# Block A's work moved off the fours, and second parts of weights given to GpSimd, in a two-block attention kernel

## The chip, the cores and the metric

The kernel runs on one core of a Trainium2 chip. The metric is the device time of one execution in microseconds. The core's engines work in parallel, each through its own instructions in order: TensorE (PE, with its weight loads PEld), VectorE (DVE), ScalarE (ACT), GpSimd (POOL) and SyncE (SP), which here issues nearly all DMAs. They wait for each other by semaphores only.

## The reference

Two attention blocks over the same shapes (2048 rows, 640 features, 32 heads of 20), whose results stand side by side:

```python
def _A_ref(x, wqkv, wo):               # local, dilated: 8 keys a row, 2 apart
    qkv = (x @ wqkv).reshape(B, S, 3, H, Dh)...
    idx = pos[:, None] - arange(8) * 2
    logits = einsum("bhsd,bhswd->bhsw", q, k[idx]) * Dh ** -0.5     # masked where idx < 0
    o = einsum("bhsw,bhswd->bhsd", softmax(logits), v[idx])
    return o @ wo
def _B_ref(x, wqkv, wo):               # full attention
    scores = einsum("bhqd,bhkd->bhqk", q, k) * Dh ** -0.5
    return einsum("bhqk,bhkd->bhqd", softmax(scores), v) @ wo
return concatenate([a, b], axis=-1)
```

All inputs and outputs are float32.

## The kernel before

**Numbers as two parts.** A matrix product of float32 operands runs as three passes over a first part (the value rounded, `act.copy` into a float32r tile) and a second part (the rest, a subtraction `raw - first`). Each weight and each piece of x is therefore split once: a cast on ACT and a `tensor_tensor` subtraction on DVE, or on GpSimd where the code says `gp`. The subtraction reads two SBUF tiles.

**Stages**, in PE's order: (1) block A's q, k, v rows (0 to 163 us). (2) The *fours* (`b_quad`, 163 to 237 us): block B's q and k for the first 1024 rows, five rounds (`m` = 0 to 4), each two column blocks by two halves of the rows with seven half products instead of eight; a round yields four results (`n` = 0 to 3), and behind each result the loop counts one group and does side work: the next round's weight pair is cast, summed and split. (3) The first V stage, 16 groups of `v_group` (237 to 274 us): block B's v rows for x's first half, half a weight (320 columns) in groups 1 to 8, the other half in 9 to 16, while x's second half is loaded (`x_pair.load`) and split (`x_pair.base`). (4) The *products* (274 to 361 us): q and k of the second 1024 rows, again five rounds `m` of two row blocks `n` and two weights `j`, 20 groups; `m_parts` splits the next round's two weights. From group 9 on a step of `b_max` stands behind each group: score products whose maxima DVE takes straight from PSUM (tile `mx`). (5) The second V stage, 14 groups with maxima too (361 to 412 us). (6) The loop over 512 steps (32 units of 16) of block B's attention (412 to 1669 us), in which PE's matmuls, ACT's exponentials and DVE's maxima follow an order written out by hand (`UNIT`); the maxima of a unit are taken 24 steps ahead of its scores. (7) The end, without maxima.

**Block A's attention** runs on GpSimd beside all this: `a_attention` is a generator of 128 pieces, and each call of `next(a_work)` issues one: a piece of scores (a product with q, `akv<-akv,aq`, then four sums and one into `al`) or one of values (`akv<-akv,al` and two sums), and the fetches (`a_fetch`, two transfers of 320 KB, and one of q where a row tile begins) for the piece two ahead; the first call fetches three. In the stages, `piece(...)` names the groups behind which a piece stands. In the loop it is every fourth step, and one more wherever `i % 96 == 33`. A finished tile of 128 rows is turned at place 9 of a unit and multiplied by A's output weight in the unit's one slot `G`.

**What else stands in the queues.** `wide_raw` loads V's half weight into three `stg` tiles (there are three in all), `wide_parts` splits it. `WPair.load` puts the pair of an odd round into the tile `aot`, that of an even one into two `stg` tiles. SP's queue holds every DMA in program order: stores of results (`qb_d`, `kb_d`, `vb_d`), loads, and block A's fetches. In the first V stage a V result is evicted by ACT into one of four `ve` tiles, which come free when their store four groups before has landed; PE has four PSUM banks for these groups. In the loop the maxima of a unit pass from DVE's turn to a split on GpSimd (`mtr`), a store and a load (`bq<-mdr`) before the next unit's scores.

Of the kernel before, what the change touches and what calls it, by code (L numbers as in the profile page):

```python
# [65 lines left out]
def attention_pair(ctx, tc, xa, wqk_a, wv_a, wo_a, xb, wqk_b, wv_b, wo_b, oa, ob):  # L66
# [142 lines left out]
            split(u[:, 0, m:m + b - a], u[:, 1, m:m + b - a], src[:, a:b], "p", second)  # L209
        return t, [lambda a=a, b=b: piece(a, b) for a, b in PAIRS]  # L210

    def wide_raw(src):

        t = [sb.tile([128, 640], F32, tag="stg", bufs=3, name="stg") for _ in PAIRS]
        raw = [u[:, :(b - a) * 320].rearrange("p (k c) -> p k c", c=320) for u, (a, b) in zip(t, PAIRS)]
        for r, (a, b) in zip(raw, PAIRS):
            sp.dma_start(r, src[:, a:b])
        return raw

    def wide_parts(raw):  # L220
        w = [sb.tile([128, KC, 320], F32R, tag="w", bufs=4, name="ww") for _ in range(2)]
        for r, (a, b) in zip(raw, PAIRS):
            act.copy(w[0][:, a:b], r)
            dve.tensor_tensor(w[1][:, a:b], r, w[0][:, a:b].bitcast(F32), ALU.subtract)
        return w

    def wide_pieces(src, second=None):
# [578 lines left out]
    groups = 0  # L806

    def piece(*at):
        if groups in at:
            next(a_work, None)  # L810

    loads = []
    for m in range(5):
        w = pairs_w.pop()
        for n, _ in enumerate(b_quad(w, x_pair)):
            tick()
            groups += 1
            piece(6, 11, 16)
            if m < 4:
                if n == 0:  # L820
                    pairs_w = [WPair(*MS[m + 1], w_raws.pop(0))]
                    pairs_w[0].base()
                    if m < 3:
                        w_raws.append(WPair.load(*MS[m + 2], m))
                elif n == 1:
                    pairs_w[0].sums()
                elif n == 2:
                    pairs_w[0].split()
            elif n == 1:
                WV = wide_parts(raw_v)  # L830
            if m == 3 and n == 3:
                raw_v = wide_raw(wv_b[0])
    low()

    def max_rows(m4, m1, q, qc):
# [365 lines left out]
    x_pair = XPair(2)  # L1201
    WV = [WV]

    def m_parts(raw):
        w = [sb.tile([128, 2, KC, 128], F32R, tag="w", bufs=4, name="w") for _ in raw]
        for u, r in zip(w, raw):
            act.copy(u[:, 0], r)
            dve.tensor_tensor(u[:, 1], r, u[:, 0].bitcast(F32), ALU.subtract)
        return w

    w_raws, WB = [], []
    for groups in range(1, 17):
        half, s = divmod(groups - 1, 8)
        v_group(s // 4, half, s)
        tick()
        if groups == 1:
            raw_v = wide_raw(wv_b[1])
        elif groups == 6:
            WV.append(wide_parts(raw_v))
        if groups in (1, 2, 3, 4, 5):  # L1220
            x_pair.load(groups - 1)
        if groups in (9, 11):
            x_pair.base(groups // 2 - 4)
        if groups in (7, 9):
            w_raws.append(WPair.load(*MS[groups // 2 - 3], groups // 2 - 3))
        if groups == 13:
            WB.append(m_parts(w_raws.pop(0)))
        piece(3, 8, 13)
# [6 lines left out]
    for m in range(5):  # L1235
        w = WB.pop()
        for n in (2, 3):
            for j in range(2):
                p = bank()
                product(p, [lambda i, k=k: w[j][:, i, k] for k in range(KC)],  # L1240
                        [lambda i, k=k: chunk(XB[n], i, k) for k in range(KC)], True, True)
                give(p)
                b_parts(p, MS[m][j], n, None, False)
                tick()
                groups += 1
                if n == 2 and j and m < 4:
                    WB.append(m_parts(w_raws.pop(0)))
                elif n == 2 and m < 3:
                    w_raws.append(WPair.load(*MS[m + 2], m))
                elif (m, n, j) == (3, 3, 0):  # L1250
                    raw_v = wide_raw(wv_b[0])
                elif (m, n, j) == (4, 2, 0):
                    WV = [wide_parts(raw_v)]
                piece(2, 5, 8, 11, 14, 17)
                if groups == 14:
                    k_loads = b_keys(0, 2, 4)
                if groups in (1, 2, 14, 15):
                    for fn in k_loads[:2]:
                        k_loads.pop(0)()
                if groups > 2 and len(q_loads) > 8:  # L1260
                    for fn in q_loads[:2]:
                        q_loads.pop(0)()
                if groups > 17 and v_loads:
                    v_piece(0, *v_loads.pop(0))
                if groups > 8:
                    for i in islice(steps, 1):
                        b_max(i)
    v_late = [(3, 1, 14), (3, 1, 15)]
    for groups in range(1, 15):
# [2 lines left out]
        tick()  # L1272
        if groups == 1:
            raw_v = wide_raw(wv_b[1])
        elif groups == 5:
            WV.append(wide_parts(raw_v))
        for i in islice(steps, 1):
            b_max(i)
        if groups > 2 and q_loads:
# [49 lines left out]
    for i in range(NS + LAG):  # L1329
# [9 lines left out]
        tick()  # L1339
        if loads and i % 2:  # L1340
            loads.pop(0)()
        if i > 14 and (i % 4 == 3 or i % 96 == 33) and next(a_work, 0) == 0:
            for d in done_a:
                d[0] -= 1
        if i % NKB == SLOT and done_a and done_a[0][0] <= 0:
# [79 lines left out]
```

## Time and profile before

| | |
|---|---|
| median of 3 runs | 1785.26 us (1784.45 to 1787.24) |
| the profiled execution | 1786.85 us, span of its trace 1785.0 us |
| busy share: PE / DVE / ACT / POOL | 98% / 79% / 76% / 69% |
| PE busy in the fours | 67.3 of 74.2 us |
| PE busy in the first V stage | 35.8 of 37.2 us |
| PE busy in the products | 82.6 of 86.5 us |
| PE busy in the second V stage | 46.1 of 51.1 us |
| PE busy in the loop | 1248.8 of 1257.0 us |
| GpSimd busy in the loop | 1073.2 of 1257.0 us |

In a timeline a row is: start in us, duration in us, engine, line, operation, out<-in by tile names, shapes, the count of equal instructions merged (their duration is then the stretch that they cover), and in brackets the engine's idle time before it with what ended it. In a list of groups a row gives the count, the busy us and the mean ns of one, and the idle time before. All instructions pass through one helper line, L61, so they are told apart by tile names: `w`, `ww` weights of B, `xn`, `xl` the parts of x, `akv` block A's fetched rows, `pr` an evicted result of q or k, `mx` maxima.

### The profile page before, as it was taken

The page shows a single profiled execution, that of the slowest core. Times are in us where ns is not written, and L with a number is a line of the kernel's source. Part 1 is how long each engine was busy: PE and PEld are TensorE (multiplying, and loading weights), DVE is VectorE, ACT ScalarE, POOL GpSimd, SP SyncE. Part 2 cuts the span into 40 slices and gives each one's busy share as a digit, 9 for nine tenths or more (in the row PEclk, how much of TensorE's full clock was granted, in tenths as well). Part 3 has the DMA queues.
Part 4 walks back from the last instruction along what each step waited for, and adds up shares of the span by engine and source line. Part 5 has one row for each costly group of instructions (what it writes and reads, how often), then busy time and mean ns, then how long its engine had stood idle before and what let it go on. Part 6 is the DMA issues. An engine that isn't in the chain of part 4 may idle for free.

```text
span 1785.0 us, 32041 instructions
## 1 busy us (share of the span) xinstructions
PE 1754.0 (98%) x11301; PEld 995.6 (56%) x11301; DVE 1410.9 (79%) x1914; ACT 1348.8 (76%) x2632; POOL 1224.8 (69%) x1080
## 2 busy tenths in 40 slices
PE   9999899989999999999999999999999999999999
PEld 8987688676444445444444444445444444444569
DVE  3115844777999999999999999999999999999400
ACT  4224233117999998999999999998999999888881
POOL 0000555533899989899898998888989899845432
PEclk9999999999999999999999999999999999999999
DMA  7574688656435653564555456545553535221223
GB/s 257 165 239 159 232 293 274 213 167 171 141 117 161 168 152 104 171 161 141 155 146 153 127 173 159 154 123 163 142 175 96 140 104 163 64 72 55 66 70 110
DMA packets 215859, 272.04 MB, mean 152 GB/s; under 512 B 91894, under 2 KB 132214, under 8 KB 215698
## 3 DMA queue, kind: packets, MB, share of 16 engines
q1 hardware_dynamic: 215122, 269.34, 50.5%
q8 instruction: 89, 1.46, 0.4%
q14 instruction: 72, 0.59, 0.1%
q10 hardware_dynamic: 576, 0.66, 0.1%
HBM read 195.17 MB, written 74.74 MB: 151 GB/s over the span
## 4 chain that ended last, share of the span: by engine, by line
PE 78%; DVE 5%; ACT 2%; DMA 1%; issue 1%; SPq 0%; POOL 0%; DVEq 0%; ACTq 0%; POOLq 0%
PE ps_st L61 78%; DVE mx L61 4%; ACT e L61 1%; DMA stg<-wv_b 1%; SPq L61 0%; DVE w L61 0%; POOL braw L61 0%; DVE ww L61 0%; DMA stg<-wqk_b 0%; ACT more L61 0%; DVE pr L61 0%; ACT pr L61 0%; DMA bq<-mdr 0%; ACT ww L61 0%; ACT w L61 0%
## 5 line engine op out<-in xcount | busy, mean ns | idle before, releaser
L61 DVE TENSOR_REDUCE mx<-ps_st 128x1 f32<-128x512 f32 (+1 forms) x1500 | 1217.7, 877 | 67.0 <-PE ps_st L61 55.8
L61 ACT ACTIVATE e<-ps_st 128x512 f32<-128x512 f32 x2048 | 1067.4, 609 | 37.4 <-PE ps_st L61 17.8
L61 PE MATMUL ps_st<-bq,bk 62*128 62x512 f32 x2048 | 610.9, 440 | 1.8 <-DMA bq<-mdr 0.9
L61 PE MATMUL ps_st<-bk,bq 60*128 60x512 f32 x2048 | 557.7, 435 | 10.3 <-DVE mx L61 10.1
L61 PEld LDWEIGHTS ps_st<-bq,bk 62*128 62x128 f32 x2048 | 288.5, 184 | 480.3 <-ACT e L61 342.9
L61 PE MATMUL ps_st<-e,vb 128*32 128x512 f32 x4096 | 542.9, 604 | 2.7
L61 POOL TENSOR_TENSOR braw<-braw,more 128x512 f32<-128x512 f32 x224 | 287.7, 1284 | 130.4 <-ACT more L61 119.6
L61 POOL TENSOR_TENSOR akv<-akv,aq 128x1280 f32<-128x1280 f32 x64 | 189.4, 2959 | 200.8 <-DVE w L61 189.4
L61 POOL TENSOR_TENSOR akv<-akv 128x640 f32<-128x640 f32 (+3 forms) x304 | 288.5, 949 | 23.8
L61 PEld LDWEIGHTS ps_st<-bk,bq 60*128 60x128 f32 x2048 | 267.3, 184 | 46.5 <-DVE mx L61 21.0
L61 ACT COPY ro<-ps_st 128x320 f32<-128x320 f32 (+2 forms) x132 | 62.5, 475 | 193.6 <-PE ps_st L61 167.3
L61 PEld LDWEIGHTS ps_st<-e,vb 128*32 128x32 f32 x4096 | 82.0, 108 | 157.3 <-issue 71.3
L61 POOL TENSOR_TENSOR akv<-akv,al 128x1280 f32<-128x1280 f32 x64 | 151.4, 2366 | 0.2
L61 ACT COPY more<-ps_st 128x512 f32<-128x512 f32 x224 | 132.5, 591 | 1.4 <-PE ps_st L61 1.4
L61 PE MATMUL ps_st<-ww,xn 128*128 128x320 f32 x768 | 126.9, 315 | 2.2 <-ACT ww L61 1.2
L61 PEld LDWEIGHTS ps_st<-ww,xn 128*128 128x128 f32 x768 | 115.3, 190 | 19.4 <-ACT e L61 8.8
L61 PE MATMUL ps_st<-wc,xn 128*128 128x512 f32 (+1 forms) x432 | 101.8, 381 | 0.0
L61 PEld LDWEIGHTS ps_st<-wc,xn 128*128 128x128 f32 x432 | 80.4, 189 | 14.1 <-ACT xn L61 0.3
L61 PE MATMUL ps_st<-xn,w 128*128 128x512 f32 x330 | 85.9, 406 | 0.7 <-ACT ro L61 0.7
L61 PE MATMUL ps_st<-ww,aot 128*128 128x320 f32 x480 | 77.8, 314 | 1.6
L61 POOL TENSOR_TENSOR ao<-ao,akv 128x640 f32<-128x640 f32 x48 | 75.3, 1570 | 3.8
L61 PEld LDWEIGHTS ps_st<-ww,aot 128*128 128x128 f32 x480 | 70.6, 188 | 10.2 <-ACT e L61 3.8
(81 smaller groups left out, 1088.3 us busy)
## 6 DMA issues: line engine op xcount, KB each, us to landing
akv<-ka_d SPq DMA_DIRECT2D x128, 320.0 KB
akv<-va_d SPq DMA_DIRECT2D x128, 320.0 KB
wx<-wa_d SPq DMA_DIRECT2D x24, 480.0 KB
kb_d<-pr SPq DMA_DIRECT2D x20, 512.0 KB
qb_d<-pr SPq DMA_DIRECT2D x20, 512.0 KB
bq<-qb_d SPq DMA_DIRECT2D x64, 160.0 KB
bk<-kb_d SPq DMA_DIRECT2D x14, 640.0 KB
rb<-s_d SPq DMA_DIRECT2D x128, 64.0 KB
```

The costliest lines, as they stand in the source:

```text
L61: return self.tc.keep_in_program_order(op(*a, **k))
```

## The change

It has four parts.

1. `piece(6, 11, 16)` in the fours is gone, so that block A's first three pieces stand in the first V stage (behind groups 3, 8 and 13, where pieces four to six stood); the products get seven pieces (behind groups 1, 4, 7, ... 19) for six (2, 5, ... 17).
2. Second parts of weights by GpSimd: `m_parts(..., gp)` for the four pairs inside the products, issued behind the first result of a round's four instead of the second (`n == 2 and not j`), the pair's load one group later; `wide_parts(..., gp)` for V's two half weights in the second V stage, its second one group earlier. V's second half weight in the first V stage stays with DVE, two groups earlier (group 4 for 6).
3. V's first half weight is asked for behind round 3's first result instead of its fourth, two of its three pieces into the tile `aot`, and split behind round 4's first result instead of its second.
4. In the loop the additional piece comes every 72 steps instead of 96.

The core of the diff:

```diff
-    def wide_raw(src):
-        t = [sb.tile([128, 640], F32, tag="stg", bufs=3, name="stg") for _ in PAIRS]
+    def wide_raw(src, other=False):
+        t = []
+        if other:
+            u = sb.tile([128, 2, 640], F32, tag="aot", bufs=1, name="stg")
+            t = [u[:, 0], u[:, 1]]
+        while len(t) < len(PAIRS):
+            t.append(sb.tile([128, 640], F32, tag="stg", bufs=3, name="stg"))
...
-    def wide_parts(raw):
+    def wide_parts(raw, e=None):
...
-            dve.tensor_tensor(w[1][:, a:b], r, w[0][:, a:b].bitcast(F32), ALU.subtract)
+            (e or dve).tensor_tensor(w[1][:, a:b], r, w[0][:, a:b].bitcast(F32), ALU.subtract)
...
-            piece(6, 11, 16)
...
-            elif n == 1:
+            elif n == 0:
                 WV = wide_parts(raw_v)
-            if m == 3 and n == 3:
-                raw_v = wide_raw(wv_b[0])
+            if m == 3 and n == 0:
+                raw_v = wide_raw(wv_b[0], True)
...
-    def m_parts(raw):
+    def m_parts(raw, e=dve):
...
-            dve.tensor_tensor(u[:, 1], r, u[:, 0].bitcast(F32), ALU.subtract)
+            e.tensor_tensor(u[:, 1], r, u[:, 0].bitcast(F32), ALU.subtract)
...
-        elif groups == 6:
+        elif groups == 4:
             WV.append(wide_parts(raw_v))
...
-                if n == 2 and j and m < 4:
-                    WB.append(m_parts(w_raws.pop(0)))
+                if n == 2 and not j and m < 4:
+                    WB.append(m_parts(w_raws.pop(0), gp))
                 elif n == 2 and m < 3:
                     w_raws.append(WPair.load(*MS[m + 2], m))
...
-                    WV = [wide_parts(raw_v)]
-                piece(2, 5, 8, 11, 14, 17)
+                    WV = [wide_parts(raw_v, gp)]
+                piece(1, 4, 7, 10, 13, 16, 19)
...
-        elif groups == 5:
-            WV.append(wide_parts(raw_v))
+        elif groups == 4:
+            WV.append(wide_parts(raw_v, gp))
...
-        if i > 14 and (i % 4 == 3 or i % 96 == 33) and next(a_work, 0) == 0:
+        if i > 14 and (i % 4 == 3 or i % 72 == 33) and next(a_work, 0) == 0:
```

**Place one: from the fours into the first V stage.** GpSimd's rows behind its last memset of stage 1 (`zero`), before:

```order
L61 MEMSET zero 7x640
L61 TENSOR_TENSOR akv<-akv,aq 128x1280
L61 TENSOR_TENSOR akv<-akv 128x2x320
L61 TENSOR_TENSOR akv<-akv 128x2x160
L61 TENSOR_TENSOR akv<-akv 128x2x64
L61 TENSOR_TENSOR akv<-akv 128x2x32
L61 TENSOR_TENSOR al<-akv 128x64
```

and of the change (`mx` and `ve` are set at the end of the fours):

```order
L61 MEMSET zero 7x640
L61 MEMSET mx_1744 128x32
L61 MEMSET mx_1745 128x32
L61 MEMSET ve 128x347 x4
L61 TENSOR_TENSOR akv<-akv,aq 128x1280
```

SP's rows in the first V stage, from the store of the second V result on, before:

```order
L61 DMA vb_d<-ve 128x336
L61 DMA stg<-xb 128x2x512
L61 DMA vb_d<-ve 128x336
L61 DMA stg<-xb 128x1024
L61 DMA akv<-ka_d 128x640 x2
L61 DMA vb_d<-ve 128x336
```

and of the change:

```order
L61 DMA vb_d<-ve 128x336
L61 DMA stg<-xb 128x2x512
L61 DMA vb_d<-ve 128x336
L61 DMA stg<-xb 128x1024
L61 DMA aq<-qa_d 128x640
L61 DMA akv<-ka_d 128x640 x6
L61 DMA vb_d<-ve 128x336
```

The first piece moved behind the memsets of `ve`, out of the fours, and its seven transfers now stand ahead of the store of the fourth V result.

**Place two: the products.** DVE's rows around the first steps with maxima, before:

```order
L61 RECIPROCAL am<-am 128x32
L61 TENSOR_TENSOR pr<-ps_st,pr 128x512
L61 TENSOR_REDUCE mx_2392<-ps_st 128x2 x2
L61 TENSOR_TENSOR pr<-ps_st,pr 128x512
L61 TENSOR_TENSOR w<-stg,w 128x640 x2
L61 TENSOR_REDUCE mx_2392<-ps_st 128x2 x2
```

and of the change:

```order
L61 TENSOR_REDUCE am<-al 128x32
L61 TENSOR_TENSOR pr<-ps_st,pr 128x512 x2
L61 TENSOR_REDUCE mx_2362<-ps_st 128x2 x2
L61 TENSOR_TENSOR pr<-ps_st,pr 128x512
L61 TENSOR_REDUCE mx_2362<-ps_st 128x2 x2
```

GpSimd's rows there, of the change (before, only pieces stand there):

```order
L61 TENSOR_TENSOR al<-akv 128x64
L61 TENSOR_TENSOR w<-stg,w 128x640 x2
L61 TENSOR_TENSOR akv<-akv,aq 128x1280
L61 TENSOR_TENSOR akv<-akv 128x2x320
L61 TENSOR_TENSOR akv<-akv 128x2x160
```

The weight's two subtractions left DVE's row between an eviction and the maxima, and stand on GpSimd between two pieces.

**Place three: the loop, unit 6** (steps 96 to 111). GpSimd's rows ahead of the split of the next unit's maxima (`mtr`), before:

```order
L61 TENSOR_TENSOR braw<-braw,more 128x512
L61 TENSOR_TENSOR al<-al,am 128x256
L61 TENSOR_TENSOR akv<-akv,aq 128x1280
L61 TENSOR_TENSOR akv<-akv 128x2x320
L61 TENSOR_TENSOR akv<-akv 128x2x160
L61 TENSOR_TENSOR akv<-akv 128x2x64
L61 TENSOR_TENSOR akv<-akv 128x2x32
L61 TENSOR_TENSOR al<-akv 128x64
L61 TENSOR_TENSOR braw<-braw,more 128x512 x2
L61 CAST mtr<-mtr 128x32
```

and of the change (`braw` sums block B's outputs):

```order
L61 TENSOR_TENSOR al<-akv 128x64
L61 TENSOR_TENSOR braw<-braw,more 128x512
L61 TENSOR_TENSOR akv<-akv,aq 128x1280
L61 TENSOR_TENSOR akv<-akv 128x2x320
L61 TENSOR_TENSOR akv<-akv 128x2x160
L61 TENSOR_TENSOR akv<-akv 128x2x64
L61 TENSOR_TENSOR akv<-akv 128x2x32
L61 TENSOR_TENSOR al<-akv 128x64
L61 TENSOR_TENSOR braw<-braw,more 128x512
L61 CAST mtr<-mtr 128x32
```

The piece right ahead of the split is the additional one of step 105, and the regular piece of step 103 ends one sum ahead of it; before, the piece ahead of the split was that of step 103, with two sums of `braw` behind it.

PE's order is the same in both programs, and so are the steps at which A's outputs are multiplied in the loop.

## The prediction

> **What bounds the kernel now.** I read the stages first (the view of busy times by stretch), then the timeline of TensorE (PE) inside each short stage, then what ran on VectorE (DVE) and GpSimd (POOL) at each gap. The page has PE busy 98% of 1785.0 us, so a shorter time must come from PE's gaps or from matmuls that run slowly behind a gap. The stages ahead of the long loop are where those are:
>
> ```profile
> 163.00:237.20 74.20, 67.32 (x270) 51.48 (x270) 57.25 (x83) 24.22 (x46) 23.44 (x22) 0.95 0.59 206
> 237.20:274.40 37.20, 35.76 (x240) 35.27 (x241) 17.91 (x20) 16.65 (x31) 26.44 (x23) 1.00 0.89 312
> 360.90:412.00 51.10, 46.07 (x274) 38.53 (x273) 37.93 (x40) 7.91 (x19) 20.05 (x23) 0.93 0.58 175
> 412.00:1669.00 1257.00, 1248.77 (x8650) 587.46 (x8649) 1199.27 (x1644) 1155.97 (x2267) 1073.19 (x936) 1.00 0.48 136
> ```
>
> Columns are the stretch, its length, then PE, weight loads, DVE, ACT, POOL, the granted clock, the DMA share and GB/s. The fours (163 to 237) leave PE idle for 6.9 us and the second V stage (361 to 412) for 5.0, both at a lowered clock; the loop leaves 8 us in 1257. So I look for the change's effect in the 250 us ahead of the loop.
>
> **The fours.** A round of the fours starts with the same six matmuls, so the distance of those rows is the length of a round:
>
> ```profile
> 175.88 1.56 PE L61 MATMUL ps_st<-xn,w 128*128 128x512 f32 x6
> ...
> 189.06 1.56 PE L61 MATMUL ps_st<-xn,w 128*128 128x512 f32 x6
> ...
> 204.06 1.56 PE L61 MATMUL ps_st<-xn,w 128*128 128x512 f32 x6
> ...
> 223.83 1.56 PE L61 MATMUL ps_st<-xn,w 128*128 128x512 f32 x6
> ```
>
> 13.18, then 15.00, then 19.77 us. Block A's three pieces run exactly in the two long rounds, and what they do to DVE stands in these rows:
>
> ```profile
> 190.76 1.29 DVE L61 TENSOR_TENSOR w<-stg,w 128x512 fp32r<-128x512 f32 x2 [0.65 <-ACT w L61]
> ...
> 207.34 3.43 POOL L61 TENSOR_TENSOR akv<-akv,aq 128x1280 f32<-128x1280 f32 x1
> ...
> 208.65 4.62 DVE L61 TENSOR_TENSOR w<-stg,w 128x512 fp32r<-128x512 f32 x2 [0.65 <-ACT w L61]
> ```
>
> The same two subtractions take 1.29 us alone and 4.62 beside a piece: a subtraction whose two inputs both lie in SBUF waits out GpSimd's instruction. Without pieces each round should be 13.18: 1.82 + 6.59 = **8.4 us saved**. V's first weight, which the change has split one group earlier in the last round, costs nothing there: rounds with a weight pair being prepared (two casts, two subtractions and more at that same place) were 13.18 as well.
>
> **V's first weight.**
>
> ```profile
> 237.57 1.90 ACT L61 CAST ww<-stg 128x640 fp32r<-128x640 f32 x3 [1.74 <-DMA stg<-wv_b]
> ...
> 238.35 0.56 PE L61 MATMUL ps_st<-ww,xn 128*128 128x320 f32 x2 [1.17 <-ACT ww L61]
> ...
> 241.21 1.92 PE L61 MATMUL ps_st<-ww,xn 128*128 128x320 f32 x12
> ...
> 274.42 2.96 PE L61 MATMUL ps_st<-xn,w 128*128 128x512 f32 x12
> ```
>
> ACT waits for the transfer of wv_b and PE for ACT. Groups 2 to 16 take (274.42 - 241.21)/15 = 2.21 us each, the first 2.86. Asked for three groups earlier into tiles that are free by then, and split a group earlier, the weight is ready: 1.17 + 0.65 = **1.8 us saved**.
>
> **Second parts by GpSimd.** In the products a group is a matrix product, then two maxima tiles per DVE step:
>
> ```profile
> 302.42 2.96 PE L61 MATMUL ps_st<-xn,w 128*128 128x512 f32 x12
> ...
> 316.39 0.50 PE L61 MATMUL ps_st<-bk,bq 60*128 60x512 f32 x2 [1.61 <-DVE mx L61]
> 317.52 0.74 PE L61 MATMUL ps_st<-bk,bq 60*128 60x512 f32 x2 [0.63 <-DVE mx L61]
> 318.18 4.36 PE L61 MATMUL ps_st<-xn,w 128*128 128x512 f32 x12
> ...
> 323.84 3.05 PE L61 MATMUL ps_st<-xn,w 128*128 128x512 f32 x12
> ...
> 328.19 2.13 PE L61 MATMUL ps_st<-xn,w 128*128 128x512 f32 x8
> ...
> 360.87 2.03 PE L61 MATMUL ps_st<-ww,xn 128*128 128x320 f32 x12
> ```
>
> An undisturbed group is 328.19 - 323.84 = 4.35 us. Groups 9 to 20 take 360.87 - 302.42 = 58.45 for 12 x 4.35 = 52.2: 6.2 too many. The row at 316.39 names DVE's maxima, and these are late because of the weight's subtractions, ahead of them on DVE:
>
> ```profile
> 311.71 3.49 DVE L61 TENSOR_TENSOR w<-stg,w 128x640 fp32r<-128x640 f32 x2
> 315.12 2.34 DVE L61 TENSOR_REDUCE mx<-ps_st 128x2 f32<-128x1024 f32 x2
> ```
>
> DVE owes 2.34 for maxima in each 4.35 us, and the low part of an eviction before them; 3.49 more doesn't fit. What stays reads PSUM and shows no slowing beside pieces (2.34 here). **6.2 us saved**. In the second V stage it is the same with V's second weight:
>
> ```profile
> 376.62 2.03 PE L61 MATMUL ps_st<-ww,xn 128*128 128x320 f32 x12
> ...
> 377.19 5.23 DVE L61 TENSOR_TENSOR ww<-stg,ww 128x640 fp32r<-128x640 f32 x3 [1.39 <-ACT ww L61]
> ...
> 383.61 0.79 PE L61 MATMUL ps_st<-bk,bq 60*128 60x512 f32 x2 [4.52 <-DVE mx L61]
> ...
> 390.25 2.03 PE L61 MATMUL ps_st<-ww,xn 128*128 128x320 f32 x12
> ```
>
> Five groups from 360.87 to 376.62 take 3.15 each, the next two 390.25 - 376.62 = 13.63: **7.3 us saved**, the slow matmuls behind the gap included. Together 8.4 + 1.8 + 6.2 + 7.3 = **23.7**.
>
> **What comes in its place.** First, block A's first piece now starts in the first V stage, with three fetches at once: seven transfers of 320 KB where there were two, ahead of the fourth V store on SP's one queue. Behind that store waits ACT's eviction, behind the evictions the casts of x, then DVE's eight subtractions, then PE at 274.42:
>
> ```profile
> 260.50 0.43 ACT L61 COPY ve<-ps_st 128x320 f32<-128x320 f32 x1 [3.62 <-DMA vb_d<-ve]
> ...
> 263.46 3.86 DVE L61 TENSOR_TENSOR xn<-stg,xn 128x1024 fp32r<-128x1024 f32 x2 [4.95 <-ACT xn L61]
> ...
> 268.12 2.61 DVE L61 TENSOR_TENSOR xn<-stg,xn 128x1024 fp32r<-128x1024 f32 x2
> ...
> 271.25 1.55 DVE L61 TENSOR_TENSOR w<-stg,w 128x640 fp32r<-128x640 f32 x2
> ```
>
> Five more transfers at this stage's 312 GB/s are 5.2 us; the stage's stores and loads start some 2 us earlier against PE, since the evictions of the last round no longer wait behind V's weight. The delay of ACT lies between 0 and 5.2; I take half, 2.6. DVE: alone the eight take 4 x 1.3 + 2 x 0.65 (half the size) + 2 x 0.78 = 8.1 us; in the trace they took 272.80 - 263.46 = 9.3, since a piece ran beside the first four alone. Now three pieces stand back to back from the fetches' landing on, so all eight run beside one:
>
> ```profile
> 274.12 2.96 POOL L61 TENSOR_TENSOR akv<-akv,aq 128x1280 f32<-128x1280 f32 x1
> ...
> 280.97 2.96 POOL L61 TENSOR_TENSOR akv<-akv,aq 128x1280 f32<-128x1280 f32 x1
> ```
>
> A piece of scores, six instructions, is 280.97 - 274.12 = 6.85 us. By the row at 263.46 each subtraction beside one loses (3.86 - 2.61)/2 = 0.6: 8 x 0.6 = 5.0, less the 1.2 that stands there now, 3.8. The first half weight was done near 272.0, 2.4 ahead of PE. So PE waits 3.8 + 2.6 - 2.4 = 4.0. Behind 2.2 us of waiting (1.61 at 316.39, 0.63 at 317.52) a product took 4.36 instead of 3.05: 1.3 more. I take **5.3**. The lower bound is 0 (no delay, no new meeting). The upper has each subtraction behind a whole GpSimd instruction, a piece and the next one's product (6.85 + 2.96 = 9.8, less 1.2), and all of the delay: 8.6 + 5.2 - 2.4 + 1.3 = 12.7. I stay nearer the lower half, since 0.6 is the row of this very subtraction.
>
> The Trainium skill speaks against the change here: SBUF — State Buffer, "Who interferes with whom", has a DVE instruction with two SBUF inputs and a GpSimd instruction that reads SBUF exclude each other, whoever is second blocking to the end. By that alone the upper 8.6 would hold and the term be near 10, the time 1772; the trace agrees in the fours (4.62 for 1.29), while the 0.6 at 263.46 lies below it. On the slow matmuls, TensorE: Matmul & The Clock Gate, "Part 1: The HAM clock gate", lets the clock fall after an idle window of about 3.4 us, by which a wait of 4.0 in pieces would often cost no ramp and the 5.3 be 4.0; the row at 318.18 shows one after 2.2, and I keep it.
>
> Second, GpSimd's queue. Its prices:
>
> ```profile
> L61 POOL TENSOR_TENSOR akv<-akv,al 128x1280 f32<-128x1280 f32 x64 | 151.4, 2366 | 0.2
> ...
> L61 POOL TENSOR_TENSOR akv<-akv 128x640 f32<-128x640 f32 x112 | 176.6, 1577 | 8.8
> ...
> L61 POOL TENSOR_TENSOR ww<-stg,ww 128x640 fp32r<-128x640 f32 x8 | 12.9, 1610 | 0.6
> ```
>
> A piece of values, a product and two sums of 640, is 2.37 + 2 x 1.58 = 5.5 us. The products' 80.2 us get 5 x 6.9 + 2 x 5.5 + 4 x 3.2 + 4.1 for V's = 62 us of GpSimd: it fits. The tight place is the second pair handed over. An estimate of where GpSimd stands: the fetches are asked for at V's third group, 6.6 us into the stage, behind V's second weight and three loads of x (2.4 MB, 7.7 us at 312 GB/s), and are 2.3 MB themselves (7.3), so the pieces start 14 to 20 us into the 37.2 and take 3 x 6.85 and half of DVE's 8.1: they end 2 to 8 us into the products. Then come the first pair (3.2), two pieces (13.7) and half of the second pair (1.6), done at 20 to 27, where PE asks for it at group 9, (302.42 - 274.42) = 28.0. Bounds 0 and 3 (the other half); I take **0.5**, near 0, since the halves are wanted one group apart. Third, the loop. It gets 115 pieces for 113, extra ones at steps 33, 105, 177, ...; each second of these falls on the step right ahead of GpSimd's split of the next unit's maxima (place three of the order). What lateness costs there:
>
> ```profile
> 521.40 0.21 DVE L61 STREAM_TRANSPOSE mtr<-mx 128x32 f32<-128x32 f32 x1
> ...
> 528.75 0.20 POOL L61 CAST mtr<-mtr 128x32 fp32r<-128x32 f32 x1
> ...
> 536.66 0.49 PE L61 MATMUL ps_st<-bq,bk 62*128 62x512 f32 x1 [0.93 <-DMA bq<-mdr]
> ```
>
> Behind the extra piece at step 33 GpSimd was 7.1 us late and PE waited 0.93, so up to 6.2 are free, and one piece is 6.9 or 5.5. Six extra pieces now, five before: between -1 (waits like this one vanish, as the pieces there are of values now) and +3 (1 us at three places); I take **0.5**.
>
> **The sum** on the profiled execution's own 1786.85 us (span 1785.0 and 1.85 around it): -23.7 + 5.3 + 0.5 + 0.5 = -17.4, 1769.4. It lies 1.6 above the median of the runs shown, 1785.26, within their spread; from the median the forecast is **1767.9**.
>
> **Rivals.** (1) Nothing new waits in the V stage and at the products' start (the train of transfers is drained in time): 1785.3 - 23.7 + 1 = 1762.6, down to 1760. For it: the stores start earlier. Against: DMA share 0.89 there already. (2) GpSimd becomes the bound in the products, since its pieces are lengthened by DVE at the start and every later pair is late by what remains: another 5 to 9 us (twice the backlog of up to 8, less what the 18 us of room give back), 1773 to 1777. For it: 62 us of 80 and that backlog. Against: the handovers behind the second come four groups of 4.35 apart, 17.4 us for one pair and at most 1.4 pieces. (3) The change doesn't do what it says in the fours, since their long rounds have another cause (206 GB/s of transfers, say): 8.4 stays, 1776.3. Against: DVE's two durations. (4) Slower: GpSimd falls behind in the loop at the three places where an extra piece now stands right ahead of the split of the maxima (steps 105, 249, 393), and the next unit's scores wait for the maxima. To eat 17.4 us each must hold PE for 5.8, so the split must be 5.8 + 6.2 = 12 us late; with both scores pieces there still queued, 13.7, it is 7.5 each, 22, and the time 1790. Against: 7.1 is what the trace shows behind an extra piece; two of the three places have pieces of values; GpSimd is idle for 184 of the loop's 1257 us.
>
> **How the numbers follow.** Forecast 0.58 (1763 to 1773), rival 1 0.16, rival 2 0.14, rival 3 0.07, rival 4 0.05. 1759.5 to 1776 takes in the first two and most of rival 2, over eight in ten. The terms' own bounds are -23.7 - 1 (1760.5) and -23.7 + 12.7 + 3 + 3 (1780); the last 4 us of that would need all three at their worst, and I leave them out. A measurement of this kernel tells 0.2% (3.6 us) from no change. Faster than that: everything but rival 4 and the tail of rivals 2 and 3, 0.91; within it 0.04; slower 0.05.
>
> **What would show it.** In the fours all rounds 13.2 us apart and no DVE w above 1.3 for two; V's first group 2.2; in the products no gap ended by DVE mx, no w or ww on DVE after the first pair; the second V stage at some 3.1 a group. A PE gap ended by DVE w or xn at the products' start, of 2 to 6 us, would show the new wait; its absence, rival 1; gaps ended by POOL w at later pairs, rival 2; units of the loop above 42 us with PE released by DMA bq<-mdr, rival 4. The forecast is wrong if the stages ahead of the loop shorten by less than 12 or more than 25 us, or if the loop from its first values product on grows by more than 3.

## The result, and the profile after

The changed kernel takes 1766.8 us (median; 1764.1 to 1772.1) beside 1785.2 for the kernel before on the same chip: a ratio of 0.990, 95% interval 0.987 to 0.992. The forecast was 1767.9, the range 1759.5 to 1776.0. The profiled execution took 1767.61 us, its span is 1765.8, so its span is 19.2 shorter than that of before. The busy times by stretch, cut at the same instructions of PE in both traces (first matmul of the fours, of the first V stage, of the products, of the second V stage, first values product of the loop, and that of unit 30 and 31), first before:

```profile
163.28:238.35 75.07, 67.32 (x271) 51.48 (x271) 57.27 (x84) 24.66 (x46) 23.44 (x22) 0.95 0.60 209
238.35:274.42 36.07, 35.77 (x240) 35.28 (x241) 17.88 (x20) 15.93 (x30) 26.46 (x23) 1.00 0.88 309
274.42:360.87 86.45, 82.57 (x350) 60.19 (x348) 51.16 (x54) 19.17 (x33) 44.69 (x34) 0.98 0.72 239
360.87:417.11 56.24, 51.21 (x307) 42.25 (x305) 40.97 (x45) 11.42 (x27) 20.15 (x24) 0.94 0.58 167
417.11:1653.69 1236.58, 1228.73 (x8523) 577.99 (x8521) 1180.98 (x1621) 1137.86 (x2231) 1060.55 (x924) 1.00 0.48 137
1653.69:1700.46 46.77, 46.03 (x316) 25.73 (x315) 17.79 (x26) 41.87 (x85) 20.45 (x21) 1.00 0.19 55
```

and after:

```profile
162.56:227.84 65.28, 64.64 (x271) 50.22 (x271) 49.29 (x87) 25.55 (x48) 0.71 (x2) 1.00 0.51 184
227.84:263.04 35.20, 35.20 (x242) 35.20 (x240) 13.68 (x13) 14.97 (x28) 15.77 (x12) 1.00 0.96 339
263.04:346.07 83.03, 80.52 (x350) 58.97 (x348) 45.90 (x49) 19.16 (x34) 72.04 (x63) 1.00 0.78 258
346.07:395.03 48.96, 48.79 (x307) 40.33 (x305) 36.30 (x41) 11.42 (x27) 25.83 (x23) 1.00 0.74 211
395.03:1631.67 1236.64, 1229.96 (x8522) 576.71 (x8521) 1182.05 (x1622) 1137.68 (x2231) 1075.37 (x939) 1.00 0.49 138
1631.67:1681.22 49.55, 47.66 (x316) 26.05 (x314) 19.40 (x26) 41.91 (x85) 20.47 (x21) 0.97 0.17 52
```

| stretch | before | after | difference | forecast |
|---|---|---|---|---|
| fours and first V stage | 111.1 | 100.5 | -10.7 | -8.4 - 1.8 |
| products | 86.45 | 83.03 | -3.4 | -6.2 + 5.3 + 0.5 |
| second V stage | 56.24 | 48.96 | -7.3 | -7.3 |
| loop up to unit 30 | 1236.58 | 1236.64 | +0.1 | +0.5 |
| unit 30 | 46.77 | 49.55 | +2.8 | none |

The last 84.5 us differ by 0.04; stage 1, which the change doesn't touch, came out 0.7 shorter. In the timeline of PE after, the rounds of the fours and the first V group stand so:

```profile
188.35 1.56 PE L61 MATMUL ps_st<-xn,w 128*128 128x512 f32 x6
...
201.53 1.56 PE L61 MATMUL ps_st<-xn,w 128*128 128x512 f32 x6
...
214.67 1.56 PE L61 MATMUL ps_st<-xn,w 128*128 128x512 f32 x6
...
227.84 1.93 PE L61 MATMUL ps_st<-ww,xn 128*128 128x320 f32 x12
...
230.04 1.92 PE L61 MATMUL ps_st<-ww,xn 128*128 128x320 f32 x12
```

Every round is 13.2 us, the V stage begins without a wait and its first group takes 2.20. At the products' start stands the new wait. PE, DVE and ACT there:

```profile
263.04 0.62 PE L61 MATMUL ps_st<-xn,w 128*128 128x512 f32 x2
266.08 2.59 PE L61 MATMUL ps_st<-xn,w 128*128 128x512 f32 x10 [2.42 <-DVE w L61]
...
269.21 2.96 PE L61 MATMUL ps_st<-xn,w 128*128 128x512 f32 x12
```

```profile
254.01 5.22 DVE L61 TENSOR_TENSOR xn<-stg,xn 128x1024 fp32r<-128x1024 f32 x2 [14.07 <-ACT xn L61]
...
265.10 4.42 DVE L61 TENSOR_TENSOR w<-stg,w 128x640 fp32r<-128x640 f32 x2
```

```profile
251.04 0.43 ACT L61 COPY ve<-ps_st 128x320 f32<-128x320 f32 x1 [7.13 <-DMA vb_d<-ve]
```

The first product takes 269.21 - 263.04 = 6.17 us for 3.49 elsewhere: 2.7 lost. ACT waited 7.13 for a store behind the seven transfers, and DVE's eight subtractions run beside pieces from 254.0 to 269.5. Two of the pieces' rows on GpSimd:

```profile
254.21 3.94 POOL L61 TENSOR_TENSOR akv<-akv,aq 128x1280 f32<-128x1280 f32 x1
...
265.31 3.53 POOL L61 TENSOR_TENSOR akv<-akv,aq 128x1280 f32<-128x1280 f32 x1
```

From group 9 on the products keep 4.35 a group but for one loss of 0.34.

The 2.8 of unit 30 were in no term. GpSimd after, then DVE after:

```profile
1639.97 1.55 POOL L61 TENSOR_TENSOR ww<-stg,ww 128x640 fp32r<-128x640 f32 x1
```

```profile
1640.02 2.05 DVE L61 TENSOR_TENSOR xl<-stg,xl 128x512 fp32r<-128x512 f32 x1
```

Before, the same two met the other way round: DVE's `xl` began 0.12 ahead of GpSimd's, took 0.69, and GpSimd's took 1.98. Whoever begins second waits: in eleven of the twelve profiles that have both instructions DVE's began first, by 0.04 to 0.27 us, and GpSimd's took 1.87 to 2.07 for 1.55; this one is the twelfth. Here 0.05 us decided, and DVE's maxima came late. PE after:

```profile
1642.73 0.49 PE L61 MATMUL ps_st<-bk,bq 60*128 60x512 f32 x1 [1.19 <-DVE mx L61]
```

Of the 2.8, some 1.2 are this wait and 1.6 are matmuls that ran more slowly in this unit, whose clock was 0.97. PE's other wait there, 0.69 for maxima, is no part of the loss, since it was 0.73 before.

### The profile page after: what moved, and what is told of

The parts are those of the page before. It is cut to its first block, busy times and chain, and to the rows that moved or that the text cites. A ratio compares the mean times of both kernels' runs of the same rounds, so it can differ in the third digit from the quotient of the medians.

```text
span 1765.8 us, 32044 instructions
## 1 busy us (share of the span) xinstructions
PE 1748.4 (99%) x11301; PEld 989.7 (56%) x11301; DVE 1391.4 (79%) x1900; ACT 1348.6 (76%) x2632; POOL 1239.4 (70%) x1094
## 4 chain that ended last, share of the span: by engine, by line
PE 86%; DVE 6%; POOL 2%; ACT 2%; DMA 2%; issue 1%; SPq 1%; DVEq 0%; POOLq 0%; ACTq 0%
PE ps_st L61 86%; DVE mx L61 5%; POOL akv L61 1%; ACT e L61 1%; SPq L61 1%; DMA vb_d<-ve 1%; DMA akv<-ka_d 0%; POOL braw L61 0%; DVE pr L61 0%; DMA bq<-mdr 0%; DVE stg L61 0%; DVE xl L61 0%; ACT more L61 0%; ACT pr L61 0%; DMA qb_d<-pr 0%
## 5 line engine op out<-in xcount | busy, mean ns | idle before, releaser
L61 POOL TENSOR_TENSOR akv<-akv 128x640 f32<-128x640 f32 (+3 forms) x304 | 284.0, 934 | 23.8
```

The source lines that it names most:

```text
L61: return self.tc.keep_in_program_order(op(*a, **k))
```

## The experiments

### Each half of the change alone

First parts 1 and 4 on the kernel before: the pieces move, the weights stay.

```diff
-            piece(6, 11, 16)
...
-                piece(2, 5, 8, 11, 14, 17)
+                piece(1, 4, 7, 10, 13, 16, 19)
...
-        if i > 14 and (i % 4 == 3 or i % 96 == 33) and next(a_work, 0) == 0:
+        if i > 14 and (i % 4 == 3 or i % 72 == 33) and next(a_work, 0) == 0:
```

> Parts 1 and 4 alone on the kernel before: no piece beside the fours, seven in the products, an extra one every 72 steps; all weights as before. Theory (the terms of the sum stand side by side and add up): the four full rounds of the fours 13.2 us apart (8.4 saved), V's first group still 2.9, a wait of PE for DVE at the products' start as in the change (2.7 there), groups 9 to 20 of the products still near 58 and the second V stage still near 51. Time 1785.3 - 8.4 + 2.7 = 1779.6, between 1777 and 1782. Rival (the long rounds of the fours come from the weights' work, not from the pieces): long rounds stay, 1785 to 1788.

Measured: 1785.2 us (1779.5 to 1790.5), ratio 0.999 (0.997 to 1.001): by the median nothing, a miss by 5.6. The ten executions lie in two groups, though: five at 1779.5 to 1783.7, four of them where the theory had the time, and five at 1786.8 to 1790.5. The profile is of one of the second group (1790.2). In it the rounds are 13.2 as expected, but the products take 96.5 us for 86.5: 4.7 more in the first product, where 2.7 had been expected, and 5.5 more in groups 9 to 20. PE there:

```profile
268.93 3.74 PE L61 MATMUL ps_st<-xn,w 128*128 128x512 f32 x10 [2.92 <-DVE w L61]
...
312.81 0.50 PE L61 MATMUL ps_st<-bk,bq 60*128 60x512 f32 x2 [2.44 <-DVE mx L61]
...
350.11 0.50 PE L61 MATMUL ps_st<-bk,bq 60*128 60x512 f32 x2 [3.37 <-DVE mx L61]
```

and DVE ahead of the two later waits:

```profile
307.30 4.32 DVE L61 TENSOR_TENSOR w<-stg,w 128x640 fp32r<-128x640 f32 x2
...
343.34 5.58 DVE L61 TENSOR_TENSOR ww<-stg,ww 128x640 fp32r<-128x640 f32 x3
```

In this execution the pieces met DVE's subtractions of weights again, now in the products (4.32 for two, where a pair alone takes 1.6), and what the fours gained went there and into the wait at the start. The five faster executions have no profile. Their median, 1780.3, is 5.4 below the kernel before, and the theory had 5.7 (8.4 - 2.7), so there the loss in the products can't have been as large. Their mean granted clock was 0.995 to 0.998, that of the others 0.992 to 0.995. The rival (the fours' rounds stay long) is out.

Then parts 2 and 3 alone: in the changed kernel the pieces go back to their old places.

```diff
+            piece(6, 11, 16)
...
-                piece(1, 4, 7, 10, 13, 16, 19)
+                piece(2, 5, 8, 11, 14, 17)
...
-        if i > 14 and (i % 4 == 3 or i % 72 == 33) and next(a_work, 0) == 0:
+        if i > 14 and (i % 4 == 3 or i % 96 == 33) and next(a_work, 0) == 0:
```

> Parts 2 and 3 alone: second parts by GpSimd, V's first weight asked for earlier; the pieces at their old places (three in the fours, six in the products, every 96 steps in the loop). Theory: fours' rounds 15.0 and 19.8 again where pieces run, V's first group 2.2, no PE wait for DVE at the products' start, products' groups 4.35 and second V stage's 3.1 from the first to the last: 1785.3 - 1.8 - 6.2 - 7.3 = 1770.0, between 1768 and 1773. Rival (GpSimd can take the second parts only because the pieces moved: with a piece behind group 2 and 5 instead of 1 and 4 a pair is late): PE gaps ended by GpSimd's w at groups 5 or 9 of the products, 3 to 7 us each, 1773 to 1780.

Measured: 1771.6 us (1770.4 to 1772.3), ratio 0.991 (0.990 to 0.993): 14.0 saved. Rounds in PE's timeline:

```profile
203.96 1.56 PE L61 MATMUL ps_st<-xn,w 128*128 128x512 f32 x6
...
223.71 1.56 PE L61 MATMUL ps_st<-xn,w 128*128 128x512 f32 x6
```

Both long rounds are there again (14.96, and the 19.75 shown), the products have 80.1 us and the second V stage 48.8, and no wait of PE for GpSimd's weights stands in the products: the rival is out. By their medians the halves give 0.4 and 14.0, 14.4 together, and the whole change 18.4: in the median the 8.4 of the fours are had only where the weights have left DVE. With the faster five executions of the first half the terms would add up (5.4 + 14.0 = 19.4).

### What made the fours' rounds long

The changed kernel with three pieces' work put back on tiles that GpSimd fills itself, so without transfers:

```diff
+            if groups == 5:
+                dummy = sb.tile([128, 2, D], F32, tag="akv", bufs=4, name="akv")
+                dq = sb.tile([128, D], F32, tag="aq", bufs=2, name="aq")
+                dl = sb.tile([128, WIN, H], F32, tag="al", bufs=2, name="al")
+                for u in (dummy, dq):
+                    gp.memset(u, 1.0)
+                a_t[-1] = [dq, dl, None]
+            if groups in (6, 11, 16):
+                a_scores(-1, 1, dummy)
```

> The changed kernel with three pieces' worth of GpSimd work added back in the fours at the old places, on tiles that GpSimd filled itself, so that no transfer belongs to it (six instructions of the same sizes each; they add to no result). Theory (DVE's subtractions wait for GpSimd's instructions): rounds of the fours are long again, DVE's pair of subtractions 3 to 5 us where it meets a piece instead of 1.3; 4 to 9 us lost there, time 1771 to 1776. Rival (transfers made them long): all rounds 13.2, time that of the change, 1766 to 1768.

Measured: 1768.9 us (1766.1 to 1770.8), all rounds 13.2. That looks like the rival, but the trace says that the experiment missed its place. GpSimd:

```profile
122.39 2.96 POOL L61 TENSOR_TENSOR akv<-akv,aq 128x1280 f32<-128x1280 f32 x1
```

With nothing to wait for, GpSimd ran these instructions in stage 1, 120 to 148 us, not beside the fours. So the work was tied to the third round by one column that it reads of a weight split there:

```diff
+            if groups == 7:
...
+                gp.tensor_copy(dq[:, :1], pairs_w[0].y[:, 1, 0, :1].bitcast(F32))
+                for _ in range(3):
+                    a_scores(-1, 1, dummy)
```

> As the run with three pieces' worth of GpSimd work added to the changed kernel and no transfers, but now the first of these instructions reads one column of the weight that DVE subtracts in the third round of the fours, so that the work starts there (near 192 us, where block A's first piece stood before) and not in the stage ahead. Theory (DVE's two-input subtractions wait for GpSimd's instructions): two rounds of the fours near 15 and 19 to 20 us again, DVE's pair of w subtractions 3 to 5 us, the V stage starting 6 to 9 us later than in the change. Rival (the transfers, or their landing, made the rounds long): all rounds 13.2.

Measured: 1781.8 us (one execution). Rounds on PE, then DVE beside the third piece:

```profile
188.92 1.56 PE L61 MATMUL ps_st<-xn,w 128*128 128x512 f32 x6
...
205.77 1.56 PE L61 MATMUL ps_st<-xn,w 128*128 128x512 f32 x6
...
226.28 1.56 PE L61 MATMUL ps_st<-xn,w 128*128 128x512 f32 x6
```

```profile
207.93 3.18 DVE L61 TENSOR_TENSOR pr<-pr 128x512 fp32r<-128x512 f32 x1
211.04 3.28 DVE L61 TENSOR_TENSOR w<-stg,w 128x512 fp32r<-128x512 f32 x2
```

Rounds of 16.9 and 20.5 with no transfer of block A: GpSimd's instructions make them, as the theory has it. (The fours are 11.0 longer than in the change, more than the 6 to 9 expected, and at the products' start PE waits 5.57.) The other way round, the kernel of the next run has the seven transfers in the fours and no piece beside them, and its rounds are 13.2.

### The wait at the products' start

Transfers of the first three pieces in the fours, the pieces where the change has them:

```diff
     def a_attention():
-        for n in range(2):
+        for n in range(3):
             a_fetch(n)
+        yield
         soft = {}
         for n, (t, c) in enumerate(UNITS):
-            a_fetch(n + 2)
+            if n:
+                a_fetch(n + 2)
...
             groups += 1
+            piece(9)
```

> The changed kernel, but the seven transfers for block A's first three pieces are issued in the fours, behind the first result of the third round, and the pieces themselves stand where the change has them. Fours: if GpSimd's instructions made the long rounds, all rounds stay 13.2; if the transfers made them, the third or fourth grows by 2 to 6.6. Products' start: in the change ACT's casts were late behind the stores and DVE's subtractions long beside pieces, and the wait of PE was 2.7. Theory (both together, 1.9 of ACT's delay and 3.5 on DVE against 2.4 of slack): without the transfers ahead of the fourth V store ACT is no longer late, and the wait falls below 1.1. Rival (DVE beside the pieces alone decides): 2 to 3 stay. Rival (the stores alone decide): 0. Time by the theory 1764 to 1766.5; 1766 to 1768 by the first rival; above 1769 if transfers lengthen the fours.

Measured: 1762.5 us (1761.7 to 1765.6), ratio 0.987 (0.985 to 0.989), some 4 below the change. PE, DVE and ACT at the same place:

```profile
263.16 2.96 PE L61 MATMUL ps_st<-xn,w 128*128 128x512 f32 x12
```

```profile
249.44 3.48 DVE L61 TENSOR_TENSOR xn<-stg,xn 128x1024 fp32r<-128x1024 f32 x2 [5.10 <-ACT xn L61]
```

```profile
241.83 0.43 ACT L61 COPY ve<-ps_st 128x320 f32<-128x320 f32 x1 [2.13 <-DMA vb_d<-ve]
```

No wait is left, the products take 80.46 us; ACT's 7.13 behind the store are gone. That is what the second rival (the stores alone decide) had, and the time is below the theory's 1764 to 1766.5. But GpSimd's pieces also ran earlier (230 to 255, since their data lie ready), so this run took both causes away. The pieces now meet the subtractions of V's second weight, for which PE doesn't wait (1.96 us in the change):

```profile
238.10 6.24 DVE L61 TENSOR_TENSOR ww<-stg,ww 128x640 fp32r<-128x640 f32 x3 [7.31 <-ACT ww L61]
```

Two more runs separate the causes. The first is the changed kernel without the first three pieces' instructions (it leaves their scores at zero, so block A's first 128 rows come out wrong), transfers as in the change:

```diff
-                a_scores(t, c, a_kv.pop(n))
+                if n > 2:
+                    a_scores(t, c, a_kv.pop(n))
```

> The changed kernel with its transfers where they are, but the first three pieces of block A without their GpSimd instructions (their scores are left out and zero in their place, so block A's first rows are not computed). At the products' start: theory (ACT late by 1.9 behind the stores and DVE longer by 3.5 beside the pieces, against 2.4 of slack): ACT's casts are still late behind the stores (a wait near 7 for the store in the V stage), DVE's eight subtractions take 8 to 9.3 instead of 15.5, and PE doesn't wait. Rival (the stores alone decide): PE still waits 2 to 3 there.

Measured: 1762.9 us (one execution). PE, DVE and ACT:

```profile
263.70 2.96 PE L61 MATMUL ps_st<-xn,w 128*128 128x512 f32 x12
```

```profile
255.16 2.36 DVE L61 TENSOR_TENSOR xn<-stg,xn 128x1024 fp32r<-128x1024 f32 x2 [14.66 <-ACT xn L61]
...
261.19 1.56 DVE L61 TENSOR_TENSOR w<-stg,w 128x640 fp32r<-128x640 f32 x2
```

```profile
252.11 0.43 ACT L61 COPY ve<-ps_st 128x320 f32<-128x320 f32 x1 [7.65 <-DMA vb_d<-ve]
```

ACT is as late as in the change, DVE's eight take 7.6 us, and PE doesn't wait: the late store alone costs nothing. And the reverse, early transfers with the pieces tied to the first cast of x:

```diff
-        piece(3, 8, 13)
+        if groups == 9:
+            mark = sb.tile([128, 1], F32, tag="mark", bufs=1, name="mark")
+            gp.tensor_copy(mark, XB[2][0][:, 0, 0, :1].bitcast(F32))
+            next(a_work, None)
+        piece(9, 13)
```

> The kernel with the first three pieces' transfers in the fours, but GpSimd's first piece starts only when ACT has cast the first part of x (one column of xn is read ahead of it), so that the three pieces run beside DVE's eight subtractions as in the change, while no store is late behind a train of transfers. Theory (the wait at the products' start needs both: with the transfers in the fours the subtractions begin near 249.5, 4.6 earlier than in the change, and 12 us of them up to the first half of the weight end at 261.5, ahead of PE's 263.2): the eight take 13 to 16 us and PE doesn't wait. Rival (meeting the pieces is enough by itself): PE waits 2 to 3 for DVE's w at the products' start.

Measured: 1767.5 us (one execution). DVE, then PE:

```profile
251.91 3.46 DVE L61 TENSOR_TENSOR xl<-stg,xl 128x512 fp32r<-128x512 f32 x1
255.29 4.42 DVE L61 TENSOR_TENSOR xn<-stg,xn 128x1024 fp32r<-128x1024 f32 x2
```

```profile
263.38 2.96 PE L61 MATMUL ps_st<-xn,w 128*128 128x512 f32 x12
...
295.09 4.14 PE L61 MATMUL ps_st<-xn,w 128*128 128x512 f32 x10 [3.08 <-POOL w L61]
```

The eight end at 262.3 (12.7 us from 249.6, just under the 13 to 16 expected) and PE doesn't wait at the start. Nor would it have if the first seven had taken the 12.0 us of the change: from 249.6 that is 261.6, ahead of 263.4. So it takes the late store and the meeting together, as the theory has it. But the 1767.5 are no gain: PE now waits 3.08 at the products' group 9, for the second pair of weights on GpSimd, whose queue the later pieces hold. That is the prediction's second rival, at one place. The change itself is not far from it. GpSimd's second pair there, and the product that asks for it:

```profile
290.83 3.10 POOL L61 TENSOR_TENSOR w<-stg,w 128x640 fp32r<-128x640 f32 x2
```

```profile
293.61 2.95 PE L61 MATMUL ps_st<-xn,w 128*128 128x512 f32 x12
```

The first half is ready at 290.83 + 1.55 = 292.4, 1.2 ahead of this row and some 1.7 ahead of its third matmul, the first that needs a second part. Had PE not lost 2.7 at the products' start, that matmul would have come 1.0 before the half was ready.

### The loop's additional piece

```diff
-        if i > 14 and (i % 4 == 3 or i % 72 == 33) and next(a_work, 0) == 0:
+        if i > 14 and (i % 4 == 3 or i % 96 == 33) and next(a_work, 0) == 0:
```

> The changed kernel with the loop's additional piece every 96 steps again. Theory (the loop's term is small, within 1): the loop up to its last unit but one within 1 us of the change's 1236.6, the time 1765 to 1768. Rival (the extra pieces ahead of the split of the maxima cost more, the waits of up to 0.3 at three places with what follows them): 2 to 3 us faster in the loop, 1763 to 1765. Another way: block A ends later with two pieces fewer, and the last steps, where its output weight gives way to block B's, come out 1 to 5 longer.

Measured: 1765.8 us (1764.8 to 1767.4), ratio 0.989 (0.987 to 0.991), as the change; the loop up to unit 30 took 1235.8 us, and unit 30 took 46.8. Six additional pieces for five cost 0.9 or less. (In one profile, that of the pieces' move alone, PE waited 1.85 for a unit's maxima in the loop; in the two of the change at most 0.30.) Its profile shows at the products' start what the change's profile doesn't. PE:

```profile
267.16 3.85 PE L61 MATMUL ps_st<-xn,w 128*128 128x512 f32 x10 [2.76 <-DVE w L61]
```

Behind a wait of nearly the same length the ten matmuls take 3.85 us for 2.59, and the first product costs 4.6 more than the next ones, not 2.7; 1.6 of this are slower matmuls. In the run with GpSimd's work in stage 1, whose program is the same at this place, it is so too (7.87 us for the first product):

```profile
266.62 4.14 PE L61 MATMUL ps_st<-xn,w 128*128 128x512 f32 x10 [2.58 <-DVE w L61]
```

### The spread, and the end

The changed kernel once more:

> The changed kernel once more, beside the two that follow, to see its own spread (1764.1 to 1772.1 in four executions) and a second profile. In the first profile the wait at the products' start was 3.0 without slow matmuls behind it, and in two kernels with the same program there (the one with work added in the stage ahead, the one with every 96 steps) 3.2 to 3.4 with them, 1.4 to 1.9 more. If that and the meeting near the end (2.8) make the spread, the runs lie between 1763 and 1770 and this profile shows one or the other of the two.

Measured: 1770.5 us (1765.7 to 1772.5), ratio 0.991 (0.989 to 0.992). Its profile is of the execution of 1765.7; PE at the products' start:

```profile
267.38 2.59 PE L61 MATMUL ps_st<-xn,w 128*128 128x512 f32 x10 [2.92 <-DVE w L61]
```

No slow matmuls here, though the profile of the pieces' move alone has them behind the same 2.92 us, and unit 30 takes 46.8: the profile shows neither of the two. The nine executions of the change lie between 1764.1 and 1772.5; the expected upper end of 1770 was too low, and none of the four above 1770 has a profile. What is on record of them is the mean granted clock: 0.998 in these four, 0.999 in the one of 1767.6, 1.000 in the four below 1766.2. By that the four lost some 2 to 5 us to a lower clock (an estimate, 0.002 of 1770 us with both clocks rounded to a thousandth), at places that no profile shows. Beside it, on the same chip, the kernel with the early transfers, and that kernel with the split of `xl` near the end on GpSimd:

```diff
-        split(chunk(o, 0, k), chunk(o, 1, k), ot_b[k * 128:(k + 1) * 128, qc * 512:(qc + 1) * 512])
+        split(chunk(o, 0, k), chunk(o, 1, k), ot_b[k * 128:(k + 1) * 128, qc * 512:(qc + 1) * 512],
+              **({} if qc else {"second": gp, "first": gp.tensor_copy}))
```

> The kernel with the transfers of the first three pieces in the fours, once more beside the change on one chip: 1762 to 1763.5, 3 to 4.5 below the change.

Measured: 1762.4 us (1762.1 to 1763.2), ratio 0.987 (0.985 to 0.988). The time is as expected. The distance to the change is not: with the change at 1770.5 on the same chip it is 8.1, where 3 to 4.5 was expected. Over all executions on record the medians are 1767.6 (nine of the change) and 1762.5 (eight with early transfers). This is the version that beats both the kernel before and the change.

> The kernel with the first three pieces' transfers issued in the fours, and in addition the split of one output chunk near the end of the loop (xl, the first quarter's fifth chunk) on GpSimd for ACT and DVE: in the change's profile DVE's one subtraction there took 2.05 us for 0.69, since GpSimd's subtraction of block B's output weight had begun 0.05 us before it, and the unit was 2.8 longer. Theory (that meeting, which happens in some executions only, is what spreads the runs of the change from 1764 to 1772): the time falls a little below that of the kernel with the early transfers (1762.5) and the runs lie within 2 us of each other. Rival (the spread has another cause): the median within 0.5 of 1762.5, the runs spread by 4 or more. Against it: GpSimd's queue is 2 us longer there, and if block B's weight is late by it, the end grows by 1 to 2.

> The same with the chunk's split near the end by GpSimd, once more on one chip with the two kernels before it: if the meeting near the end matters in one execution of several, 0.3 to 1 below the kernel without it and a narrower spread; otherwise the same within 0.5.

Measured: 1762.1 in both (1761.1 to 1762.5 and 1761.1 to 1763.3), ratios 0.987 (0.985 to 0.988) and 0.987 (0.985 to 0.988). Its 0.3 to 0.4 below the kernel without that edit can't be told from nothing. Of the eight executions with early transfers alone one took 1765.6 and seven 1761.7 to 1763.2, so most of the change's spread went with the wait at the products' start. The slow matmuls behind that wait (1.6) and the meeting near the end (2.8, in one profile of the twelve that have both instructions) are part of it; whether they make all of the 1770 to 1772 stays open.

## Why the prediction was right

**Fours, 8.4, and V's first weight, 1.8:** right in place and size (10.7 with the first V stage), and right in cause: the run with work and no transfers has the long rounds, the run with transfers and no work doesn't. Rival 3 is out.

**Products' maxima, 6.2:** 58.45 became 346.07 - 293.61 = 52.46 for groups 9 to 20, 6.0. **Second V stage, 7.3:** 7.3.

**The new wait, +5.3 forecast, 2.7 in the profile.** The mechanism was right, its sizes were not. ACT's delay: DVE began 9.0 us ahead of PE's need for 11.0 before, 1.9 for the assumed 2.6. DVE: the subtractions that PE waits for took 12.0 for 8.5, 3.5 longer for the forecast 3.8, but by errors that cancel. The price of 0.6 for each was too low: the eight took 15.5 where the run without the pieces' work has 7.6, so nearly 1.0 each. Of these 7.9, 1.7 lay in the trace of before already (forecast 1.2). And PE waits only for seven of them, not eight: the eighth's 2.7 cost nothing. 1.9 + 3.5 - 2.4 is 3.0, and 0.3 of it is covered by the product's first two matmuls, which need no second part.

So the Trainium skill's rule (SBUF — State Buffer, "Who interferes with whom": a DVE instruction with two SBUF inputs and a GpSimd instruction that reads SBUF exclude each other) was nearer for DVE than my row: by the pieces' length it made 9.8 of lengthening (8.6 beyond the 1.2 of before), 7.9 was measured, against 5.0 by the row. The term stayed far from the 10 of that rule mostly because the eighth subtraction isn't waited for (2.7), because the lengthening was 1.9 smaller, and because the ramp, the 1.3 for slow matmuls behind the wait, was absent in the profile.

That ramp is half of the difference between 5.3 and 2.7. In two other kernels whose program is the same at this place it is there (1.5 and 1.6), and the whole term 4.4 and 4.6. On this the Trainium skill, in TensorE: Matmul & The Clock Gate, "Part 1: The HAM clock gate", has an idle window of about 3.4 us that runs free, so that the cold stretch varies from run to run. The rows agree with the second half: matmuls were slow behind 2.58, 2.76 and 2.92 (the last with the pieces' move alone), not behind 2.42 and 2.92. The first half they don't bear out, since all three slow ones followed a pause shorter than the window.

**GpSimd's second pair, +0.5:** 0 in the change, since PE had been held 2.7 just ahead of it. The margin was 1.2, and the run with later pieces crossed it. The half was estimated done 20 to 27 us into the products and was done after 29.4: beside DVE's subtractions the second and third piece took 11.1 and 7.9 us for 6.85, and GpSimd was busy for 72.0 us of the products, for the 62 forecast. I had priced the two terms apart; they are not independent.

**The loop, +0.5:** 0.1. The one wait for a unit's maxima in the loop is 0.3 us; rival 4 didn't come.

**What was left out:** unit 30. No term spoke of it, since the change doesn't touch it, and 2.8 were lost there in the profiled execution, where 0.05 us decided a meeting of two instructions. From profiled execution to profiled execution the time fell by 19.2 for the 17.4 forecast; without this loss it would have been 22.0. That the forecast stands so near is luck in part: this loss hides most of what the smaller wait at the products' start (2.6), GpSimd's 0.5 and stage 1's 0.7 took off. From its first values product on the loop, with the end, grew by 2.9, just under the 3 that the prediction had named as a sign of being wrong. Of the rivals, the first (nothing new waits, 1762.6) is what the kernel with early transfers measures, 1762.5.

The terms were added as if each could be had alone. The runs of one half each show that this is not safe: by its median the pieces' move alone is worth nothing, and in its profiled execution it meets in the products the very subtractions that the other half takes away. In its executions near 1780 the term came out as added; why these differ is not shown.

## What to carry to other kernels

Work moved off one stage is to be priced by what it meets in the next, and with the other edits in place: where instructions of two engines shut each other out, as here, the loss can move with the work to the next stage. Where a stage's stores share a queue with prefetches, try the prefetch in the stage before, even if the work on it stays (here ACT's wait of 7.13 went, and the fours stayed as short). And a wait that is taken away should be priced together with the next margin behind it, which may be as thin as the wait was long.

## What was not expected of the hardware

The exclusion goes by who starts first: one pair of instructions near the end cost GpSimd 0.3 to 0.5 us in eleven profiles (1.98 for 1.55 before) and DVE 1.4 in the twelfth (2.05 for 0.69), as one or the other was ahead by as little as 0.04 or 0.05 us. And matmuls behind a pause of 2.4 to 2.9 us at the products' start were slow in three profiles and not in two others, in no order of the pause's length: behind 2.92 both are on record.
